# A decode block on one core: weights and caches laid out in sixteen lines, and a pick matmul with 512 moving columns

## The chip, the core and the metric

The kernel runs on one core of a Trainium2 chip. A core has a tensor engine (PE in the profile; PEld is its weight load), a vector engine (DVE), a scalar engine (ACT), a general engine (POOL) and a sync engine (SP), which here issues the DMA transfers. Sixteen DMA engines carry data between device memory (HBM) and the on-chip memory SBUF, which has 128 partitions. Matmul results go to PSUM.

The metric is the device time of one execution in microseconds; lower is better.

## The reference

Two branches work on the same normalised input and are added to it: attention of one new token over the last 2048 positions of a cache, and a gated bilinear feed-forward. Batch 2, width 512, 32 heads of 128, feed-forward width 1376, everything in 32-bit floats.

```python
xn = layernorm(x)                                   # x: [2, 1, 512]
q = (xn @ wq).reshape(2, 1, 32, 128).transpose(0, 2, 1, 3)
k, v = k_cache[:, :, -2048:], v_cache[:, :, -2048:] # of 8192 positions
p = softmax(einsum("bhqd,bhkd->bhqk", q, k) * 128 ** -0.5)
o = einsum("bhqk,bhkd->bhqd", p, v)
A = o.transpose(0, 2, 1, 3).reshape(2, 1, 4096) @ wo
h = (xn @ w_gate) * (xn @ w_up)
out = x + A + h @ w_down
```

With one token for each of two batch rows every weight and every cache entry is used once, so 159 MB have to come from HBM.

## The kernel before

**The array.** On the host, `laid_out` (line 773) arranges all weights and the used part of the caches into one array of 128 rows, `stream`, one row for each SBUF partition. A row holds the parts of 26 loads one behind the other: `loads` names them in order of issue, and `lines` (line 113) gives each load its start in the row, rounded up to `LINE` = 128 elements, and makes the row's length an odd number of such lines. A load's source is therefore a block of 128 rows and so many columns; between one partition's part and the next lies a whole row of the array (1,246,720 bytes, from the widths in the code):

```python
rows = stream.rearrange("(p i) -> p i", i=total)
src[name] = rows[:, starts[name] : starts[name] + hi - lo]
```

**The ring.** In SBUF all loads go into one tensor, `ring` (called `step` in the profile), with fixed places: one place for a group's V (`C_V`), one for a group's K (`C_K`), and between them places for wq and wo. There are 8 groups (`NG`) of 4 heads (`HG`). A group's K load and its V load have 16,384 columns each, 64 KB in a partition, 8 MB in all. The other loads are `x0` (7652 bytes in a partition) and `x1` (44,724), with the gate, up and first query weights; `w1` (58,880) and `w4` (65,536) with the later query, output and down weights; the last group's V in three pieces (`v28`, `v30`, `v31`); and `d0`, `wo7`, `d1`, `d2` at the end, 2048 to 8192 bytes in a partition, with down and output weights.

**The order.** `issue` (line 497) puts a load on SP's DMA queue. SP runs through them in a fixed order, each waiting until its place in the ring is free: group g+1's K is issued once the scores of group g are done (line 721), and group g+1's V once the weighing of group g is done (line 748). So while one of the two is being used, the other is on its way. A transfer that carries its own semaphore count is waited for by the first matmul that reads it.

**A group's work.** PE projects the group's queries (`project`: four 128x2 by 128x512 matmuls), DVE turns them (`queries`), and PE computes 64 score pieces into `s_ps` (`scores`). DVE, PE and ACT make the softmax weights (`maxima`, `weights`), PE weighs V into `o_ps` (`weigh`), with a sum of the weights (`tot`) between. Then `gather` (line 637) brings the 32 rows of `o_ps` together: DVE masks and adds them into `red`, and a matmul with the 0/1 matrix `pick` (128x8, columns 0 to 7 of `cst`) turns the result and picks the 8 columns of the group, one for each head and batch row:

```python
pe.matmul(pk, red, pick, start=True, stop=True)          # pk: 128 x 8 in PSUM
dve.tensor_tensor(oT, pk, rec, op=ALU.mult, tag="oT")
```

`pk` is the first 8 columns of a PSUM bank of its own, `pk_ps` (line 482). DVE multiplies by the reciprocal sums into `oT`, and `wo` (line 689) multiplies `oT` with the group's output weights into `acc` and `acc2`, which DVE adds into `xr`. PE's program is a hand-written loop over the groups (`steer`); each PE instruction waits on semaphores that count the other engines' results (`hold`). POOL copies a group's output weights from their waiting place into `C_O` and passes semaphores on (`relay`).

**The end.** In the last group PE also multiplies three rows of down weights (section `r`, from `d0`), then `gather(7)`, `wo(7)` (from `wo7`), the last three strips of down weights (from `d1` and `d2`) and `xr` itself through `id4` into a 128x128 piece of `s_ps`, which DVE copies out and SP stores.

## Time and profile before

| | us |
|---|---|
| median of three runs | 376.38 |
| lowest and highest | 375.45, 376.48 |
| the profiled execution's own time | 375.21 |
| its span, first to last instruction | 373.8 |

The profile is of one execution, which was quicker than the median run. Its span leaves out 1.4 us around the first and the last instruction. The mean granted clock of PE in it was 0.836 of full speed.

The profile page has a first part with each engine's busy time, a second with the span cut in 40 slices, where a digit 9 means nine tenths busy or more, a third with the DMA queues, and a fourth with the chain of work that ended last. The chain can also be read in order of time: a row there says when a piece started, how long it was and what it was; a DMA piece lasts from its issue to its landing. All instructions that go through the kernel's recording helper have the same line number, L133, so groups are told apart by the tiles that they write and read. Matmuls in 32-bit floats run as two passes, so that two rows stand for one `matmul` of the code. In rows of stretches of the span, each engine's busy time and count is followed by the granted clock, the DMA engines' share and GB/s.

### The profile page before, as it was taken

To read this page: it belongs to the slowest core of one execution; us is meant where nothing else is said; L and a number is where in the kernel's file an instruction comes from. 1 tells how busy PE (TensorE), PEld (TensorE's weight loads), DVE (VectorE), ACT (ScalarE), POOL (GpSimd) and SP (SyncE) were. 2 spreads that over 40 slices of the span, in tenths; PEclk is the share of its full clock that TensorE was granted. 3 is DMA by queue.
4 is the path that set the end of the run, shared out by engine and by line. 5 is a ranking of instruction groups with operands and counts; after the bars stand their busy time and mean duration, and the time that the engine had idled before them with its cause. 6 is when DMAs were issued, how large, how long until landed. Compare 5 with 4: busy or idle time off the path is not lost.

```text
span 373.8 us, 3210 instructions
## 1 busy us (share of the span) xinstructions
PE 215.1 (58%) x1362; PEld 53.4 (14%) x1362; DVE 62.7 (17%) x161; ACT 15.9 (4%) x31; POOL 15.5 (4%) x38
## 2 busy tenths in 40 slices
PE   0688770097828780776154414637662877095765
PEld 0011110022102110221011100102110211021221
DVE  3000141012120212021202010202120122003203
ACT  5011110000000000000000000000000000000000
POOL 2000000022000200000000200000200020000000
PEclk9989997568986898699869585859896889689999
DMA  8999899999899999989999999899999989999996
GB/s 335 495 449 442 365 428 491 427 449 435 358 442 449 449 449 449 449 351 435 449 449 449 449 449 414 372 449 449 449 449 449 442 365 428 449 449 393 435 419 276
DMA packets 3892, 159.54 MB, mean 427 GB/s; under 512 B 434, under 2 KB 562, under 8 KB 1076
## 3 DMA queue, kind: packets, MB, share of 16 engines
q1 hardware_dynamic: 3888, 159.54, 98.9%
q10 hardware_dynamic: 4, 0.00, 0.0%
HBM read 159.47 MB, written 0.07 MB: 427 GB/s over the span
## 4 chain that ended last, share of the span: by engine, by line
DMA 70%; PE 27%; DVE 1%; ACT 1%; issue 1%; SPq 0%; ACTq 0%
DMA step<-in_stream_dram 70%; PE o_ps L133 14%; PE q_ps L133 8%; PE s_ps L133 3%; PE acc L133 1%; ACT step L133 1%; PE tot L133 1%; DVE qt L133 1%; DVE red L133 0%; DVE om L133 0%; PE pk L133 0%; SPq L133 0%; ACT qz L133 0%; DVE oT L133 0%; ACTq L302 0%
## 5 line engine op out<-in xcount | busy, mean ns | idle before, releaser
L133 PE MATMUL o_ps<-step,p 128*32 128x512 f32 x512 | 71.5, 698 | 57.5 <-DMA step<-in_stream_dram 56.3
L133 PE MATMUL s_ps<-step,qz 128*8 128x512 f32 x512 | 60.6, 628 | 29.1 <-DMA step<-in_stream_dram 22.2
L133 PE MATMUL q_ps<-step,xn 128*2 x112 | 58.7, 674 | 16.5 <-POOL none L133 10.5
L133 PEld LDWEIGHTS o_ps<-step,p 128*32 128x32 f32 x512 | 17.0, 122 | 94.2 <-DMA step<-in_stream_dram 59.8
L133 PEld LDWEIGHTS s_ps<-step,qz 128*8 128x8 f32 x512 | 14.2, 93 | 75.6 <-issue 64.9
L133 POOL COPY step<-step 128x2048 f32<-128x2048 f32 x6 | 11.3, 1889 | 181.9 <-PE acc L133 181.9
L133 PEld LDWEIGHTS q_ps<-step,xn 128*2 128x2 f32 x112 | 9.9, 93 | 61.2 <-issue 61.2
L133 DVE TENSOR_REDUCE mt<-s_ps 128x1 f32<-128x512 f32 x8 | 5.5, 692 | 77.0 <-PE s_ps L133 77.0
L133 PE MATMUL acc<-step,oT 128*2 128x256 f32 x128 | 10.9, 469 | 11.6 <-POOL none L133 8.4
L133 DVE RECIPROCAL rec<-tot 128x8 f32<-128x8 f32 x8 | 1.7, 208 | 73.0 <-PE tot L133 73.0
L133 DVE TENSOR_TENSOR xr<-xr,acc 128x256 f32<-128x256 f32 (+1 forms) x17 | 7.4, 437 | 38.5 <-PE acc L133 38.4
L133 PE MATMUL acc<-step,hT 128*2 128x512 f32 (+1 forms) x10 | 3.3, 995 | 17.7 <-DMA step<-in_stream_dram 17.7
L133 DVE STREAM_TRANSPOSE qt<-q_ps 32x128 f32<-32x128 f32 x28 | 8.6, 306 | 24.8 <-PE q_ps L133 24.5
L133 DVE TENSOR_TENSOR om<-o_ps,cst 128x512 f32<-128x512 f32 x7 | 4.8, 691 | 36.8 <-PE o_ps L133 36.8
L133 PE MATMUL pk<-cst,red 128*128 128x8 f32 x16 | 3.3, 276 | 13.1 <-DVE red L133 13.1
L133 ACT COPY qz<-qt 128x8 f32<-128x8 f32 x8 | 1.6, 204 | 207.9 <-DVE qt L133 207.9
L133 PE MATMUL top<-dg,ones 128*128 128x32 f32 x16 | 3.3, 286 | 10.3 <-DVE dg L133 10.3
L133 ACT ACTIVATE p<-t,zero 128x128 f32<-128x128 f32 x8 | 4.2, 522 | 93.9 <-DVE t L133 93.9
L133 DVE TENSOR_REDUCE red<-om 128x128 f32<-128x512 f32 x7 | 7.1, 1019 | 0.2
L133 DVE TENSOR_TENSOR step<-step 2x1376 f32<-2x1376 f32 x1 | 1.6, 1580 | 32.2 <-ACT step L133 32.2
L133 POOL MEMSET none<- 128x1 f32 x18 | 1.6, 98 | 101.4 <-DMA step<-in_stream_dram 76.9
L133 DVE STREAM_TRANSPOSE sT<-s_ps 128x512 f32<-128x512 f32 x8 | 5.7, 709 | 0.0
(56 smaller groups left out, 55.6 us busy)
## 6 DMA issues: line engine op xcount, KB each, us to landing
step<-in_stream_dram SPq DMA_DIRECT2D x1, 7360.0 KB, 26.7
step<-in_stream_dram SPq DMA_DIRECT2D x1, 5590.5 KB, 17.4
step<-in_stream_dram SPq DMA_DIRECT2D x1, 4096.0 KB, 23.0
step<-in_stream_dram SPq DMA_DIRECT2D x1, 3072.0 KB, 27.7
step<-in_stream_dram SPq DMA_DIRECT2D x2, 1024.0 KB, 25.8
step<-in_stream_dram SPq DMA_DIRECT2D x1, 956.5 KB, 4.6
step<-in_stream_dram SPq DMA_DIRECT2D x1, 768.0 KB, 20.2
step<-in_stream_dram SPq DMA_DIRECT2D x1, 512.0 KB, 23.1
```

The source lines that it names most:

```text
L133: return getattr(engine, self.method)(*args, **self.kw)
```

## The change

Two edits, which don't depend on each other.

*The array has 16 lines instead of 128 rows.* `SHARE` is 8, the number of partitions that a line holds. For each load a line holds 8 partitions' parts one behind the other, without gaps; loads start at multiples of 128 elements in the line, as they did in the row. The source of a load becomes a block of 16 lines by 8 parts by so many columns. The destination in `ring` is unchanged. The host code that fills the array changes with it; the host's work is no part of the time.

*The pick matmul moves its 8 columns 64 times.* The moving operand is `pick` with a step of 0 over 64 repeats, 512 columns, and the result fills the whole PSUM bank `pk_ps`. DVE reads the first 8 columns, as before.

```diff
-RUNS = 7
+RUNS, TIMES = 7, 64
...
-LINE = 128
+LINE, SHARE = 128, P // 16
...
     for name, (lo, hi) in placed()[1].items():
         starts[name] = at
-        at += -(-(hi - lo) // LINE) * LINE
+        at += -(-SHARE * (hi - lo) // LINE) * LINE
     return starts, at + LINE * (1 - at // LINE % 2)
...
+    pks = pk_ps[:, 0 : TIMES * N].rearrange("p (r n) -> p r n", n=N)
...
     for name, (tag, _, _) in loads().items():
         lo, hi = spans[name]
-        src[name] = rows[:, starts[name] : starts[name] + hi - lo]
+        share = rows[:, starts[name] : starts[name] + SHARE * (hi - lo)]
+        src[name] = share.rearrange("q (n i) -> q n i", n=SHARE)
...
         pr.hold("red", g + 2, "turn")
-        pe.matmul(pk, red, pick, start=True, stop=True)
+        pe.matmul(
+            pks, red, pick.unsqueeze(1).to_broadcast([P, TIMES, N]), start=True, stop=True
+        )
         dve.tensor_tensor(oT, pk, rec, op=ALU.mult, tag="oT")
...
-    stream = np.zeros((P, total), a.dtype)
+    stream = np.zeros((P // SHARE, total), a.dtype)
     for name, (_, _, fields) in loads().items():
-        at = starts[name]
-        for kind, i in fields:
-            part = field(kind, i)
-            stream[:, at : at + part.shape[1]] = part
-            at += part.shape[1]
+        part = np.concatenate([field(kind, i) for kind, i in fields], axis=1)
+        part = part.reshape(P // SHARE, -1)
+        stream[:, starts[name] : starts[name] + part.shape[1]] = part
```

## The prediction

> **What bounds the kernel now.** I read the page's shares first, then the chain of work that ended last, then the DMA issues, then the timeline of the last 12 us.

> ```profile
> span 373.8 us, 3210 instructions
> PE 215.1 (58%) x1362; PEld 53.4 (14%) x1362; DVE 62.7 (17%) x161; ACT 15.9 (4%) x31; POOL 15.5 (4%) x38
> DMA  8999899999899999989999999899999989999996
> q1 hardware_dynamic: 3888, 159.54, 98.9%
> HBM read 159.47 MB, written 0.07 MB: 427 GB/s over the span
> ```

> Tensor work covers 58% of the span, the DMA engines 98.9%. All loads stand on one queue, and no slice but the last falls below eight tenths. So the question is whether the stream can run faster, start earlier, or end closer to the last instruction. The chain of waits in order of time gives the stream's speed:

> ```profile
> 0.73 0.38 SPq L133
> ...
> 1.17 17.40 DMA step<-in_stream_dram
> ...
> 87.75 25.64 DMA step<-in_stream_dram
> ...
> 123.49 28.59 DMA step<-in_stream_dram
> ...
> 161.64 29.14 DMA step<-in_stream_dram
> ...
> 199.84 48.99 DMA step<-in_stream_dram
> ...
> 257.88 29.65 DMA step<-in_stream_dram
> ...
> 314.74 30.84 DMA step<-in_stream_dram
> ...
> 347.65 23.11 DMA step<-in_stream_dram
> 370.76 0.04 issue
> 370.81 1.10 PE s_ps L133 x32
> ```

> The columns are start, length, what. The rows from 123.49 to 257.88 end where a V load has landed: 123.49 + 28.59 = 152.08, then 190.78, 248.83, 287.53. Between two of them lie a K and a V load of 8 MB each (4 heads x 4096 columns x 4 B x 128 partitions = 8.389 MB), 16.78 MB in 38.70 us: 433.5 GB/s, in the first and the third interval alike; the middle one holds w4 as well, 25.17 MB in 58.05 us, again 433.5. That is 27.1 GB/s for each of 16 engines, to three digits in every cycle, so I take it as a ceiling that the order of rows in memory doesn't lift.

> At that rate 159.47 MB take **367.9 us**. The first load is issued at 0.73 and the last lands at 370.76: 370.0 us. Everything that a better stream could win is 370.0 - 367.9 = **2.1 us**, and part of that is the fixed time of a first transfer. Ahead of the stream lie 0.7 us, behind it 373.8 - 370.8 = 3.0 us.

> **The layout, part by part.** The bytes, the 26 loads, their order, places in SBUF and semaphores stay. The source of a load was 128 rows at the pitch of a whole row; now it is 16 lines, and in each the rows of 8 partitions lie one behind the other, closed up. The destination is the same 128 rows.

> ```profile
> step<-in_stream_dram SPq DMA_DIRECT2D x1, 956.5 KB, 4.6
> step<-in_stream_dram SPq DMA_DIRECT2D x16, 30.3
> out_dram<-red SPq DMA_DIRECT2D x1, 64.0 KB, 1.5
> 0.00:18.60 18.60, 6.42 (x8) 0.85 (x8) 4.48 (x11) 5.01 (x7) 2.65 (x16) 1.00 0.99 417
> ```

> - *The sixteen K and V loads* (134 of 159 MB): each partition's row is 64 KB and already one run. They move at the ceiling now: gain 0, and I see no cost as long as each engine keeps a way into SBUF to itself (rival B).
> - *The short-row loads*: x0, 956.5 KB, takes 4.6 us to land. Its bytes at the ceiling are 0.979 MB / 433.5 GB/s = 2.26 us, which leaves 2.34. The store of 64 KB takes 1.5 us with 0.15 us of bytes, so about 1.35 us is what any transfer costs here. The rest, 1.0 us, is slow beginning over short rows that lie far apart. Laid end to end they may lose none or all of that: gain 0 to 1.0, and I take the middle, **-0.5 us**. That this reaches the end needs no further step: the queue is never empty, so what the front saves, the last landing saves. The other short loads stand at the end: from the landing of K7 (314.74 + 30.84 = 345.58) to 370.76 lie 25.2 us for 11.01 MB, 25.4 at the ceiling. Nothing is lost there now, so nothing is to be won.
> - *A loss of the same kind*: x0's and x1's rows (7652 and 44724 B) now begin at odd places inside a line. The stretch that holds them runs at 417 GB/s for 18.6 us, 7.76 MB, 17.9 us at the ceiling: 0.7 us is what this stretch loses now. If closed-up rows lose as much again, +0.7. From nothing in the trace can I choose more.
> - *The issue*: a source with one dimension more. An issue takes 0.38 us in the chain's second piece; twice that is +0.4 for x0, which nothing hides. For all later loads it is hidden: K7 waits 30.84 us from issue to landing with 8.389 MB / 433.5 GB/s = 19.35 us of bytes, so 11.5 us behind other loads; V1 (25.64) 6.3, the others between. I take 0.

> **The pick matmul.** It stands in every one of the eight groups, between the sum of the heads and the output projection.

> ```profile
> 339.19 3.60 PE L133 MATMUL q_ps<-step,xn 128*2 x8
> 10.54 6.42 PE L133 MATMUL q_ps<-step,xn 128*2 x8 [10.54 <-POOL none L133]
> 367.98 0.39 PE L133 MATMUL pk<-cst,red 128*128 128x8 f32 x2
> 368.41 0.17 DVE L133 TENSOR_TENSOR oT<-pk,rec 128x8 f32<-128x8 f32 x1 [0.54 <-PE pk L133]
> 369.51 1.05 PE L133 MATMUL acc<-step,oT 128*2 128x256 f32 x16 [1.14 <-DMA step<-in_stream_dram]
> 370.19 0.85 DVE L133 TENSOR_TENSOR xr<-xr,acc 128x256 f32<-128x256 f32 x2 [1.03 <-PE acc L133]
> 371.24 0.40 PE L133 MATMUL s_ps<-xr,cst 128*2 128x128 f32 x8
> ```

> Two passes take 0.39 us now (timeline of the last group). A pass over the about 500 columns of the projection takes 3.60 / 8 = 0.45 us late in the run and 6.42 / 8 = 0.80 at its beginning. The widened pick has 512 columns in two passes: 0.9 to 1.6 us, so **+0.5 to +1.2** for each group, 4 to 10 us of tensor time in all.

> In groups 0 to 6 it delays what is queued behind it: on PE the output projection, the next group's queries and scores; on DVE oT and the sums into xr; on POOL the copy of the next wo; on SP the next K load, which waits for those scores. None of it moves the stream while that K load is issued before the queue is dry, and it is issued 11.5 us early by the row of K7, V loads at least 6.3. Cost **0**; were this cover gone, +0.5 to +1.2 times seven groups.

> In group 7 it ends at 368.37; oT follows to 368.58, and the projection starts only at 369.51, when its weights have landed: 0.93 us of cover. Behind that the sums into xr end at 371.04 and the matmul that takes them starts at 371.24, 0.2 more. At 0.45 us a pass the whole +0.5 is hidden; at 0.80, 1.2 - 0.93 - 0.20 leaves +0.1. I take **0**.

> **The sum** against the profiled execution's own 375.21 us (span 373.8 and 1.4 around it): -0.5 + 0 + 0 = 374.7. The three runs' median, 376.38, stands 1.17 above that execution (they go from 375.45 to 376.48). I carry the -0.5 over to the median: **375.9 us**. Working bounds: -1.0 from x0, +0.7 + 0.4 + 0.1 from rows, issue and pick: 375.4 to 377.6.

> **The rivals.**

> *A, the end runs at the full tensor clock in every run: 374.8.* The tail behind the last landing is 1.10 us of PE work. The granted clock by stretches of the span:

> ```profile
> 200.00:258.00 58.00, 25.64 (x158) 6.14 (x158) 6.49 (x18) 0.73 (x2) 2.22 (x5) 0.71 1.00 433
> 362.00:373.80 11.80, 7.09 (x88) 2.31 (x88) 3.30 (x9) 0.00 (x0) 0.00 (x0) 1.00 0.75 305
> ```

> The last three columns are granted clock, DMA share and GB/s. In this execution the tail had 1.00; elsewhere the mean falls to 0.71. A tail at half clock would take 1.10 us more, about the 1.17 by which the median stands above this execution. If the usual run has a cold tail, and 0.5 us or more of extra matmul 3 us before the end keeps it warm, 1.1 goes on top of the 0.5: 376.38 - 1.6 = 374.8. For it: the size fits. Against: PE is busy 7.09 of the last 11.8 us already, and no row shows a cold tail. [...]

> *B, two engines meet at one way into SBUF: slower, 560 to 744.* The load now has 16 outer items on one side and 128 partitions on the other. If one line goes to one engine, as the change has it, an engine writes 8 neighbouring partitions, where today's split may be another. The steady 27.1 GB/s per engine shows that today no two share a way that is narrower than both. If the new split sends pairs down one way, each pair moves in step what one engine moved: + 367.9, 744; if pairs drift to half overlap, + 184, 560. It decides at once and in all 26 loads, from the point where two engines write through one way at the same time. For it: 16 items against 128 is a form that no load or row of before has. Against: each engine still moves as many bytes to as many partitions, and pairs that fall out of step stop meeting. [...] No row here shows which partitions an engine has.

> *C, the pick shows at the end: 377.0.* Cold passes in the last group with no gain in x0: 376.38 + 0.1 from above, and half of the tail's 1.10 on top, +0.5, if the clock that made the pick slow is still down when the tail begins.

> *D, no effect: 376.4.* The rows of an engine are fetched one by one as before, and the longer pick is hidden.

> **How the numbers follow.** Chances: my forecast with its bounds 0.48, A 0.18, B 0.12, C 0.07, D 0.15. A measurement of this kernel can tell about 0.3%, 1.1 us, so "faster" begins below 375.25: A nearly whole, and the low edge of the forecast (x0 wins all, 0.06) give 0.23. "Slower" begins above 377.5: B, half of C and the upper edge of the forecast (0.02), 0.17. The rest, 0.60, is no difference. The range leaves out B and the outer edges: 374.6 (A with a little) to 377.6 (the upper bound).

> **What will show it.** V landings still 38.70 us apart, and 433 GB/s in the middle, say that the ceiling and each engine's way in are untouched; 60 us or more say B. x0's landing below 4.6 us, near 3.6, shows the front's gain; the last landing must move by as much. The pick at 0.9 to 1.1 us with oT still ahead of wo's landing shows that it is hidden; a projection in group 7 released by DVE instead of DMA shows C. A's mark is a median at the profiled execution's level, with the tail at 1.00. I am wrong above all if the engines' shares of SBUF change, which no row of before lets me see.

## The result, and the profile after

Median 775.83 us (773.11 to 776.17, six runs) against 375.49 us for the kernel before in the same comparison; ratio 2.0645, 95% interval 2.0615 to 2.0675. The time has doubled. The profiled execution took 774.55 us, its span is 773.2.

The page of the kernel after, engines' shares, slices and DMA queues:

```profile
PE 237.6 (31%) x1362; PEld 54.3 (7%) x1362; DVE 62.6 (8%) x161; ACT 15.9 (2%) x31; POOL 15.5 (2%) x38
...
DMA  9999999999989999999999899999999999999997
GB/s 199 209 210 217 217 211 195 200 217 217 214 173 210 217 217 217 193 193 210 217 217 214 183 200 217 217 217 200 186 210 217 217 214 186 197 217 217 190 203 180
DMA packets 3892, 159.54 MB, mean 206 GB/s; under 512 B 434, under 2 KB 562, under 8 KB 1076
...
q1 hardware_dynamic: 3888, 159.54, 99.4%
...
HBM read 159.47 MB, written 0.07 MB: 206 GB/s over the span
```

The same number of packets with the same bytes, and the DMA engines as busy as before: 99.4% of the span against 98.9%. PE, DVE, ACT and POOL ran as many instructions as before; PE's are longer (237.6 us against 215.1) at a mean granted clock of 0.66 instead of 0.84. So nothing starved the DMA engines; each packet took a little more than twice as long: in the trace's packet records a packet of 64 KB, one partition's row of a K or V load, takes 5.11 us in the median instead of 2.42. Here is the trap of a busy share: engines whose packets take 5.11 us instead of 2.42 count as just as busy.

The timeline of the kernel after, first matmuls on V (start, length, what, and idle time before with its releaser):

```profile
234.09 3.64 PE L133 MATMUL o_ps<-step,p 128*32 128x512 f32 x16 [29.73 <-DMA step<-in_stream_dram]
315.02 3.64 PE L133 MATMUL o_ps<-step,p 128*32 128x512 f32 x16 [29.23 <-DMA step<-in_stream_dram]
395.97 3.40 PE L133 MATMUL o_ps<-step,p 128*32 128x512 f32 x16 [28.73 <-DMA step<-in_stream_dram]
```

They begin when a V load has landed, 80.93 and 80.95 us apart where it was 38.70, for the same 16.78 MB: 207 GB/s, 13.0 for each of 16 engines instead of 27.1. That rate accounts for practically the whole loss: 159.47 MB at 207.3 GB/s are 769 us, and the last landing stands at 769.32.

### The profile page after: what moved, and what is told of

It reads as the page before. It is cut to its first block, busy times and chain, and to the rows that moved or that the text cites. A ratio compares the mean times of both kernels' runs of the same rounds, so it can differ in the third digit from the quotient of the medians.

```text
span 773.2 us, 3210 instructions
## 1 busy us (share of the span) xinstructions
PE 237.6 (31%) x1362; PEld 54.3 (7%) x1362; DVE 62.6 (8%) x161; ACT 15.9 (2%) x31; POOL 15.5 (2%) x38
## 2 busy tenths in 40 slices
DMA packets 3892, 159.54 MB, mean 206 GB/s; under 512 B 434, under 2 KB 562, under 8 KB 1076
## 3 DMA queue, kind: packets, MB, share of 16 engines
q1 hardware_dynamic: 3888, 159.54, 99.4%
HBM read 159.47 MB, written 0.07 MB: 206 GB/s over the span
## 4 chain that ended last, share of the span: by engine, by line
another core or an unknown queue 65%; PE 21%; DMA 10%; DVE 2%; issue 1%; ACT 0%; SPq 0%; POOL 0%; POOLq 0%; ACTq 0%
DMA step<-in_stream_dram 10%; PE s_ps L133 7%; PE q_ps L133 6%; PE o_ps L133 6%; PE acc L133 1%; PE pk L133 1%; DVE red L133 1%; DVE om L133 0%; DVE mt L133 0%; ACT step L133 0%; PE tot L133 0%; PE top L133 0%; DVE qt L133 0%; DVE mtt L133 0%
## 5 line engine op out<-in xcount | busy, mean ns | idle before, releaser
L133 PE MATMUL o_ps<-step,p 128*32 128x512 f32 x512 | 75.5, 731 | 194.3 <-DMA step<-in_stream_dram 194.3
L133 PE MATMUL s_ps<-step,qz 128*8 128x512 f32 x512 | 74.9, 751 | 179.1 <-DMA step<-in_stream_dram 179.1
L133 PE MATMUL q_ps<-step,xn 128*2 x112 | 54.5, 632 | 35.2 <-ACT step L133 24.6
L133 PEld LDWEIGHTS o_ps<-step,p 128*32 128x32 f32 x512 | 16.9, 127 | 233.8 <-DMA step<-in_stream_dram 196.9
L133 PEld LDWEIGHTS s_ps<-step,qz 128*8 128x8 f32 x512 | 15.2, 104 | 238.9 <-issue 238.9
L133 DVE TENSOR_REDUCE mt<-s_ps 128x1 f32<-128x512 f32 x8 | 5.5, 691 | 241.3 <-PE s_ps L133 241.3
L133 PE MATMUL acc<-step,hT 128*2 128x512 f32 (+1 forms) x10 | 3.3, 993 | 65.4 <-DMA step<-in_stream_dram 65.4
L133 PE MATMUL acc<-step,oT 128*2 128x256 f32 x128 | 11.2, 483 | 33.3 <-POOL none L133 28.7
L133 POOL COPY step<-step 128x2048 f32<-128x2048 f32 x6 | 11.3, 1889 | 372.6 <-PE acc L133 372.6
L133 DVE RECIPROCAL rec<-tot 128x8 f32<-128x8 f32 x8 | 1.7, 208 | 204.9 <-PE tot L133 204.9
L133 DVE TENSOR_TENSOR xr<-xr,acc 128x256 f32<-128x256 f32 (+1 forms) x17 | 7.4, 437 | 108.3 <-PE acc L133 108.3
L133 PEld LDWEIGHTS q_ps<-step,xn 128*2 128x2 f32 x112 | 9.4, 89 | 76.1 <-issue 76.0
L133 PE MATMUL pk<-cst,red 128*128 128x512 f32 x16 | 10.4, 737 | 13.1 <-DVE red L133 13.1
L133 DVE STREAM_TRANSPOSE qt<-q_ps 32x128 f32<-32x128 f32 x28 | 8.6, 307 | 21.8 <-PE q_ps L133 21.5
L133 ACT COPY qz<-qt 128x8 f32<-128x8 f32 x8 | 1.6, 204 | 401.8 <-DVE qt L133 401.8
L133 ACT ACTIVATE p<-t,zero 128x128 f32<-128x128 f32 x8 | 4.2, 521 | 258.3 <-DVE t L133 258.3
L133 DVE TENSOR_TENSOR om<-o_ps,cst 128x512 f32<-128x512 f32 x7 | 4.8, 691 | 37.4 <-PE o_ps L133 37.4
L133 DVE TENSOR_REDUCE red<-om 128x128 f32<-128x512 f32 x7 | 7.1, 1019 | 0.2
L133 PE MATMUL top<-dg,ones 128*128 128x32 f32 x16 | 3.3, 286 | 10.3 <-DVE dg L133 10.3
L133 PEld LDWEIGHTS acc<-step,oT 128*2 128x2 f32 x128 | 3.0, 92 | 44.0 <-POOL none L133 29.5
L133 POOL MEMSET none<- 128x1 f32 x18 | 1.6, 98 | 205.1 <-DMA step<-in_stream_dram 183.5
L133 DVE STREAM_TRANSPOSE sT<-s_ps 128x512 f32<-128x512 f32 x8 | 5.7, 708 | 0.0
## 6 DMA issues: line engine op xcount, KB each, us to landing
step<-in_stream_dram SPq DMA_DIRECT2D x1, 956.5 KB, 7.6
```

Source lines behind the costliest of these rows:

```text
L133: return getattr(engine, self.method)(*args, **self.kw)
```

## The experiments

Theory W: with 16 outer items on the source side a load is dealt out so that each engine writes 8 neighbouring partitions, and two engines meet at one way into SBUF. Theory H: the reads are slow, because the rows of eight partitions are closed up and the engines read at other distances in HBM. Both are guesses that the runs have to decide: no view names the partitions that an engine writes. The third suspect is the pick matmul.

**Each part alone.** First the kernel before with the wide pick:

```diff
...
-        pe.matmul(pk, red, pick, start=True, stop=True)
+        pe.matmul(
+            pks, red, pick.unsqueeze(1).to_broadcast([P, TIMES, N]), start=True, stop=True
+        )
```

> The kernel before with the wide pick alone (512 moving columns, array in 128 rows). All theories: the pick takes 0.9 to 1.6 us for its two passes instead of 0.39 and is hidden in groups 0 to 6; ratio to before 0.997 to 1.002 (374.4 to 376.2 us). If the wide pick had a part in the doubling, or lay on the path in every group, 379 to 385 us.

Measured: 375.24 us, ratio 0.9997, interval 0.9988 to 1.0006. No difference. The timeline of its last group:

```profile
368.12 1.13 PE L133 MATMUL pk<-cst,red 128*128 128x512 f32 x2
369.29 0.17 DVE L133 TENSOR_TENSOR oT<-pk,rec 128x8 f32<-128x8 f32 x1 [1.28 <-PE pk L133]
...
369.63 1.04 PE L133 MATMUL acc<-step,oT 128*2 128x256 f32 x16 [0.38 <-DMA step<-in_stream_dram]
...
371.36 0.40 PE L133 MATMUL s_ps<-xr,cst 128*2 128x128 f32 x8
```

The pick takes 1.13 us instead of 0.39, and the projection is still released by its weights' landing, with 0.17 us left (oT ends at 369.46). The pick is out of the case.

**The same array in 32 lines.** One constant of the kernel after is changed, and the pick is the old one:

```diff
-LINE, SHARE = 128, P // 16
+LINE, SHARE = 128, P // 32
...
```

> The new array without the wide pick, in 32 lines of 4 partitions instead of 16 of 8: rows closed up in the same way, source of 32 x 4 items against 128 partitions. Theory W (two engines write through one way into SBUF, because 16 outer items give each engine 8 neighbouring partitions): 32 outer items can be dealt out four partitions at a time as the 128 rows of before can, so about 375 us, V landings 38.7 us apart. Theory H (the reads are slow because the rows are closed up and the engines read at other distances in HBM): 700 to 800 us still. If W holds but 32 items are also dealt out in neighbours (two lines for an engine), about 775 us, which would leave W and H both standing.

Measured: 375.77 us, ratio 1.0015, interval 1.0006 to 1.0024. Its timeline:

```profile
114.07 3.64 PE L133 MATMUL o_ps<-step,p 128*32 128x512 f32 x16 [6.51 <-DMA step<-in_stream_dram]
152.77 3.64 PE L133 MATMUL o_ps<-step,p 128*32 128x512 f32 x16 [9.70 <-DMA step<-in_stream_dram]
191.47 3.48 PE L133 MATMUL o_ps<-step,p 128*32 128x512 f32 x16 [10.52 <-DMA step<-in_stream_dram]
```

38.70 us again, to the hundredth. Rows closed up by fours cost nothing at 64 KB a row. They win nothing either: the chain of this kernel begins

```profile
0.73 0.65 SPq L133
...
1.43 17.78 DMA step<-in_stream_dram
```

The first issue takes 0.65 us where it took 0.38, and x0 lands later, not sooner:

```profile
step<-in_stream_dram SPq DMA_DIRECT2D x1, 956.5 KB, 5.3
```

That is 5.3 us against 4.6; the stretch of the first 18.6 us moves 392 GB/s against 417. From there on all stands 0.65 us later, to the last landing at 371.40 (before 370.76).

**The old rows in HBM, in 16 groups.** The kernel before, with 512 bytes of padding after every eighth row, so that a source can't be written as 128 rows of one pitch:

```diff
...
-    rows = stream.rearrange("(p i) -> p i", i=total)
+    rows = stream.rearrange("(q i) -> q i", i=SHARE * total + LINE)[:, 0 : SHARE * total]
+    rows = rows.rearrange("q (n i) -> q n i", n=SHARE)
...
-        src[name] = rows[:, starts[name] : starts[name] + hi - lo]
+        src[name] = rows[:, :, starts[name] : starts[name] + hi - lo]
...
```

> The kernel before with its old rows in HBM, 128 at the old distance, but with 512 B of padding after every eighth, so that a load's source is 16 x 8 items and can't be written as 128. Theory W: 775 us, V landings about 80 us apart, as after, although nothing in HBM has moved by more than 8 KB. Theory H: 375 us, 38.7 us apart, since each partition's row is read from where it was.

Measured: 773.7 us, ratio 2.0613, interval 2.0575 to 2.0650.

```profile
233.99 3.64 PE L133 MATMUL o_ps<-step,p 128*32 128x512 f32 x16 [29.55 <-DMA step<-in_stream_dram]
315.05 3.64 PE L133 MATMUL o_ps<-step,p 128*32 128x512 f32 x16 [29.14 <-DMA step<-in_stream_dram]
```

81.06 us apart. Theory H falls as it was put: with the rows practically where they always were, 16 outer items alone double the time (773.7 us), and with the rows closed up, 32 outer items don't (375.77). A form of it is left: the dealing may also change which rows of HBM are read at the same time, and these might be what meets. The packets of the run in four lines, below, speak to that.

**Out of step.** If it is a meeting of two engines, it should depend on when they come. Two loads more, of four rows from each of 4 lines and four from each of 12, are meant to let the engines that get both or one of them lead their partners; that they do, and which engines those are, is an estimate of mine that no view shows. They go ahead of all others into V's place, 64 KB a row; the array is in 16 lines, with the old pick:

```diff
...
+    for q, first in ((4, 64), (12, 16)):
+        at = starts["k1"]
+        junk = rows[0:q, at : at + 4 * HG * CK].rearrange("q (n i) -> q n i", n=4)
+        pr.load("SP", ring[first : first + 4 * q, C_V : C_V + HG * CK], junk)
     issue("x0")
...
```

> [...] 4.2 MB more are loaded. Theory W in the form that a pair collides only while it is in step: in the stretch from 30 to 70 us well over 217 GB/s, up to 433, until the leading engines run out of work, after which the pairs may fall into step again; the whole anywhere from 400 to 780 us. If pairs are halved whatever their phase (a fixed partner, or HBM): 217 GB/s from the start and about 790 us.

Measured: 721.05 us in one run, 55 less than after although it loads 4.2 MB more. Stretches of its span (length, each engine's busy time and count, granted clock, DMA share, GB/s):

```profile
60.00:70.00 10.00, 8.96 (x16) 1.27 (x14) 0.00 (x0) 0.83 (x2) 0.00 (x0) 0.81 1.01 367
80.00:90.00 10.00, 7.14 (x27) 1.26 (x28) 4.01 (x8) 2.29 (x4) 0.00 (x0) 1.00 0.90 288
...
140.00:200.00 60.00, 25.58 (x159) 6.17 (x151) 8.05 (x21) 0.73 (x2) 4.11 (x6) 0.70 0.99 223
200.00:300.00 100.00, 34.59 (x226) 8.93 (x226) 8.47 (x21) 0.73 (x2) 2.09 (x3) 0.66 1.00 214
```

The first 40 us, in which the two loads ahead are still under way, run at 181 to 231 GB/s. Then, with the same array in the same 16 lines, up to 367 GB/s, which fits pairs that are apart. In the trace's packet records half of the 64 KB packets that begin between 60 and 80 us (55 of 104) take 2.42 to 2.51 us, the pace of before (65,536 B at 27.1 GB/s are 2.42). Later the engines have no packet for 6% of their time from 80 to 90 us and for 9% from 140 to 150; I take it that those that had got ahead run dry and start again with the others, which no view shows. From 200 us on the rate is 214 to 221 GB/s, little above that of after (202 to 210 in stretches of 100 us). With every engine halved, 13.55 GB/s of the 27.1, no stretch would have shown more than 217 for long.

**Who meets whom.** The array in 4 lines of 32 partitions and in 2 of 64 (`P // 4`, `P // 2`, old pick), so that, if an engine takes one line, only four and two engines carry the load:

> The new array without the wide pick in 4 lines of 32 partitions: four outer items, so four engines carry all, with partitions 0-31, 32-63, 64-95 and 96-127. Theory W with partners 32 partitions apart: engines 0 and 1 meet, and 2 and 3, all the way through: each at half of 27.1 GB/s, or a little less as in the 16 lines (80.95 us for 16.78 MB is 207 GB/s, 13.0 for an engine), 4 x 13.0 = 52 GB/s, 159.5 MB in 3070 us. If partners are 16 or 64 partitions apart, or an engine's long way through its line is what costs, as Theory H would have it, either 4 x 27.1 = 108 GB/s and 1480 us (no two meet) or another figure than that of two lines.

> The same in 2 lines of 64 partitions: two engines carry all, with partitions 0-63 and 64-127. Theory W with partners 32 apart: no two engines meet, each runs at its full 27.1 GB/s, 2 x 27.1 = 54 GB/s, 2950 us: as long as with four engines, or a little shorter. If partners are 64 apart: 2 x 13.0 = 26 GB/s, 6100 us. Theory H: half or less of whatever four lines give.

Measured, in one run each: 1730.86 us with four engines, 2950.31 with two. From the page the GB/s row and the DMA queue's, first of four lines and then of two:

```profile
GB/s 64 62 64 62 64 68 62 68 70 74 75 74 80 85 85 89 95 103 106 109 109 109 109 109 106 109 109 109 106 109 109 109 109 108 108 109 109 107 104 72
...
q1 hardware_dynamic: 3576, 159.53, 24.9%
```

```profile
GB/s 52 55 53 55 53 55 54 54 55 53 55 53 55 53 55 53 55 53 55 53 55 53 55 54 54 54 54 55 53 55 53 55 53 55 53 55 53 54 54 51
...
q1 hardware_dynamic: 3524, 159.53, 12.5%
```

The shares of 24.9% and 12.5% of 16 engines are what four and two engines come to that are busy all the time (25.0% and 12.5%): here the outer count is the number of engines.

Four engines, a line of 32 partitions for each, begin near half rate (62 to 64 GB/s; four free ones would move 108). Two, with lines for partitions 0-63 and 64-127, move 52 to 55 in every slice but the last, 27.1 each, and the forecast of 2950 us was met. So, by the rates, two engines 64 partitions apart didn't meet, and in four lines some did; I read that as partners 32 partitions apart, though no view names the two that meet. The time of four lines was wrong in both forms that I gave (3070 and 1480): the rate goes from 62 to 64 GB/s up to 109 within some 800 us, as of pairs that meet at first and then drift apart by themselves, until nothing is lost.

**Does the drift need a long round?** In 16 lines nothing drifted (173 to 217 GB/s in every slice of after). If a way serves four partitions and an engine takes one line, a pair takes turns on 8 ways in 4 lines of 32 partitions and on 2 in 16 lines of 8; that is an estimate from the rhythm above. 8 lines of 16 partitions (`P // 8`), 4 ways for a pair, lie between:

> [...] In 4 lines the pairs met at first (62 to 64 GB/s) and drifted apart within 750 us (109 GB/s); in 16 lines they stayed in step to the end. If pairs drift apart whenever nothing brings them together again: 108 GB/s at first, up to 217 later, 800 to 1300 us in all. If a round of few ways holds them in step, as it would be in 16 lines (two ways): 104 GB/s to the end, 1480 to 1560 us. If no two meet: 740 us from the start.

Measured: 1416.44 us in one run, in none of the ranges.

```profile
GB/s 109 111 104 107 109 106 107 107 113 106 109 109 109 107 113 115 109 111 115 109 111 115 119 119 115 117 117 115 115 119 119 119 130 120 120 119 131 155 102 51
```

It begins at half (109 GB/s; eight free engines would move 217) and rises far more slowly than four lines. By that estimate of 8, 4 and 2 ways, a pair stayed in step the better the fewer there were, in one run each of 4 and of 8 lines. Why, the runs don't show.

**The count that can be dealt out.** 64 lines (`P // 64`, old pick), and the whole change with 32 lines and the wide pick:

> 64 lines of 2 partitions, no wide pick. Theory W: what counts is whether the outer items can be dealt out so that an engine keeps one way; 64 items of 2 rows can be, as 32 of 4 were: 375 to 377 us, V landings 38.7 us apart. If 32 was a lucky number and the rule is another: 700 us and more.

> The whole change with one constant mended: 32 lines of 4 partitions, and the wide pick. Theory W: both parts are hidden, and the longer first issue stays: 375.4 to 376.2 us, ratio 1.000 to 1.003. If the two parts need each other to do harm: more than 380.

Measured: 375.68 us, ratio 1.0012 (1.0001 to 1.0023), and 375.72 us, ratio 1.0014 (1.0005 to 1.0023). Both stand within 0.3% of before, on the slower side by about what the first issue and x0 cost. No version was measurably faster than the kernel before.

## Why the prediction was wrong

**The step that failed** is the first term of the layout: "I see no cost as long as each engine keeps a way into SBUF to itself". The condition was named, its price was worked out as rival B, and it was given 12 in 100; so the range ended at 377.6. The runs fit that 16 outer items break exactly this condition: 16 groups over the old rows give 773.7 us, 32 lines over the new array 375.8. The trace names no engine's partitions; that 16 items give each engine eight neighbours, and that two engines then meet, is inferred from these two, from the loads that set pairs apart, and from four and two lines with their busy engines and their rhythm of four rows.

What made B likelier than I held it stood in the diff. It makes as many lines as there are DMA engines (`P // 16` partitions in each), and if each engine takes one line, a destination of 128 partitions in order gives it eight neighbours. Whether eight neighbours put two engines on one way, no row of before could tell; the runs of four and of two lines came to that later (62 to 64 GB/s for four engines at first, 54 for two). I weighed against it that each engine moves as many bytes to as many partitions, which says nothing on whether two engines meet, and that pairs might fall out of step. That they can fits four lines (from 62 to 109 GB/s) and the loads ahead (up to 367); that they would in 16 lines was hope, and the slices of after are as flat at the end as at the beginning (199 to 217 GB/s in the first five, 180 to 217 in the last five).

B's price was 744 us in step; measured are 775.8. The missing 32 us are nearly all one thing: a pair in step takes a little more than double. 80.95 us against 2 x 38.70 = 77.40 is 4.6%, and 367.9 x 2 x 1.046 = 770 us of stream. B's price came so close because it had the doubling; it missed the 4.6%. The price for pairs at half overlap, 560 us, was not seen.

**The other steps**, tested apart from B:

- *The ceiling of 433.5 GB/s* that the order of rows doesn't lift: right. 38.70 us in the 32 lines too.
- *x0's gain of 0.5 us*: wrong in sign. In 32 lines x0 lands 0.7 us later from its issue, of which 0.27 is the longer issue. Closing the short rows up by fours won nothing of what x0 loses beyond its bytes and a fixed time; what that loss is, no run shows. The bounds (0.4 for the issue, 0.7 for rows) held: 0.65 in all. But the 0.7 was misread: the stretch that "loses" it is counted from 0.00, and the first load is issued only at 0.73, so its 0.7 us say nothing of rows.
- *The issue with one more dimension*: 0.65 to 0.68 us instead of 0.38 for x0, near the +0.4 named; I had put it at 0, though I had written that nothing hides it. The issue of a single K or V load takes 0.54 instead of 0.33.
- *The pick*: right in size in seven of eight groups (+0.74 us in group 7, forecast 0.5 to 1.2; group 1 of the wide pick alone took 1.96 us against 0.45, beyond the forecast), right that it is hidden, and right about the row to look at. It is closer than I had it: 0.17 us of cover are left, because a lone pair of passes takes 1.13 us, where I had put two at the pace of a long row of them, 0.90.
- *Rival A*, a tail that is cold in the usual run: wrong. Beside the wide pick alone the kernel before has a median of 375.28 us over 21 runs, and the pick's is 375.24. The 376.38 that I started from was the upper side of three runs, not the usual time; what makes the rare runs near 376.4 (2 of these 21) longer, no run shows. Nor does any show that extra matmul near the end keeps the clock up, which A's 1.1 us needs: the runs' mean granted clock is 0.813 to 0.845 with the wide pick and 0.808 to 0.840 without it, and the two rare runs' 0.813 stands beside 375.24 and 375.26 us as well.
- *Chances*: 17 in 100 for slower. The part that should have been larger is B's.

## What to carry to other kernels

A DMA's outermost count was part of its cost here: with 128, 64 and 32 outer items the loads moved 427, 426 and 426 GB/s over the span, with 16 they moved 206, with the same bytes and rows of the same length. That the count bears on which engine writes which partitions is my reading of the runs. Leave partitions outermost in a plain 128-row source, and when a layout changes the outer count, run that one load alone first. A busy share of 99% says nothing about speed (98.9% at 375 us, 99.4% at 776); bytes per engine and microsecond do, and a row of the rate as it was makes the change visible in one line.

## What the runs showed of the hardware that I had not expected

- Two engines in step on one way, as the 16 lines are read here, lose more than half: 13.0 GB/s each instead of 13.55. With the old rows it is nearly the same (81.06 us between V landings against 80.95).
- In four lines the packets' times have a rhythm of four rows, at 44,724 bytes a row (2.74, 3.31, 3.31, 2.36 us) and at 65,536 (4.27, 4.82, 4.82, 2.94) alike.
- The rate of few lines rises in the course of a run, as of pairs that drift apart: in 4 lines from 64 to 109 GB/s within about 800 us, in 8 lines from 109 to between 119 and 131 in 1270 us (one later slice of 35 us has 155), one run for each, and in 16 lines not at all in 770 us.
- Where no engines meet, each moves 27.1 GB/s whether 2 or 16 of them run (54 GB/s in 2 lines, 433 in 128 rows): up to 433 GB/s HBM doesn't show as a limit.
- A source with one more dimension costs SP 0.3 us more for the first issue (0.65 to 0.68 against 0.38) and 0.2 us more for a K or V load (0.54 against 0.33).
